# Side-by-side main and left keys, one softmax chain of 320 columns, and left outputs made once per group of four segments

## Chip, cores, metric

The kernel runs on 1 core of one Trainium2 chip. The metric is the device time of one execution in microseconds (us), as the median over several executions. The kernel before took 1781.87 us (median of 3 executions, 1777.33 to 1792.37).

## What is computed

Two branches of a transformer layer over 2048 rows of width 1024 are summed with the input: a recurrent attention over segments of 32 rows with a memory of 8 rows (A), and a dense layer with a gelu (B). Cut to what matters:

```python
def _A_ref(x, mem0, Wq, Wk, Wv, Wo, seg_len):         # x: 1 x 2048 x 1024, 32 heads of 128, M = 8, seg_len = 32
    mask = (idx[:, None] < M) | (idx[:, None] >= idx[None, :])
    mem = mem0
    for s in range(n_seg):                            # 64 segments, one after the other
        h = concat([mem, x[:, 32 * s:32 * s + 32]])   # 40 rows
        q, k, v = h @ Wq, h @ Wk, h @ Wv              # per head
        p = softmax(where(mask, q @ k.T * Dh ** -0.5, -1e9))
        o = (p @ v) @ Wo
        mem = o[:, :M]                                # goes into the next segment
        outs.append(o[:, M:])
    return concat(outs)

def _B_ref(x, w1, b1, w2, b2):                        # 1024 -> 3584 -> 1024
    return gelu(x @ w1 + b1) @ w2 + b2

return x + _A_ref(layernorm(x), ...) + _B_ref(layernorm(x), ...)
```

The memory makes the 64 segments a chain: a segment cannot start before the one ahead has given its 8 memory rows.

## The kernel before

**Two stages.** The first 340 us or so make the layer norm, branch B and, for each segment, its transposed rows in device memory. The rest of the span is the loop over 64 segments (`for s in range(NSEG)`), and all that the change touches at run time lies there.

**Rows of a segment.** A segment has 40 rows: 8 memory rows and 32 of its own. The kernel keeps 32 of them as *main* rows (24 own rows and the 8 memory rows, tile `hr_home`), since 32 rows fill one of four column groups of TensorE. The last 8 own rows are *left* rows. They don't depend on the memory, so those of four segments (a *group*; `GRP = 4`, `i4 = s % 4`) are put together to 32 rows (tile `hrL`) and projected once for the group.

**Weights.** Wq, Wk, Wv, Wo are cut into 64 units of 128 x 2048 (512 KB each): 8 for each half `u` of the heads of K, Q and V, and 16 of O. 47 stay in SBUF. 17 are streamed in each segment: 15 by DMA from device memory (`Wc_...`, issued by SP in `start_stream`, six buffers) and two that VectorE copies from PSUM (L273). `PLACED` fixes at which places of a segment's order of 64 units the streamed ones stand, one row of it for each `i4`. A buffer's next transfer is issued when its unit is done (`unit_done`).

**Products.** `half_pass` runs the eight units of one of the six halves, K0 Q0 K1 Q1 V0 V1, in this order. `product` (L830) sends a unit through TensorE as four matmuls of 512 columns, each with a stationary tile of 128 x 32 on its own column group; below this is called one *step*. A left projection adds a step to each unit of its half. Which segment has which left projection is in `left_k`, `left_q`, `left_v`. `o_product` (L1089) does the output projection: one step for each of the 16 O units, or two where left outputs are made as well (`left_o`: segments with `i4 == 1`, and the last one). In these, `left_outs` holds the left rows of four segments, two of the group ahead and two of this one (`og, slot = divmod(s + 2, GRP)`).

**Attention**, twice in a segment (`u` = 0, 1), its parts placed by hand between the units (`SCORES_0`, `SUMS_0`, `ATTEND`, `VALUES_0`, `SUMS_1`, `VALUES_1` give the unit behind which a part is issued):

- `scores`: 16 matmuls of main keys (L947) and 16 of left keys (L953), stationary 128 x 32, into two areas of one PSUM bank (`mixed`).
- `exps`: ScalarE's exp over 160 + 64 columns (L970 in one, or L966 and L967), then VectorE's minimum with two masks (L977, 96 and 64 columns).
- `sums`: eight matmuls with 0/1 columns `bd` (L985, L991), stationary 128 x 32; then on ScalarE ln of 160 columns (L996) and exp(-x) twice with two biases `off` (L999), which makes the two blocks of the 320 columns; then VectorE's products (L1012 for 320 columns, L1017 or L1024 for the left keys).
- `values`: 32 matmuls with stationary 64 x 128 (L1039, L1045), then copies out of PSUM (L1058).

**End of a segment.** `put_mem` (L320, stationary 128 x 128) turns the memory rows, VectorE copies them into the next segment's `hr_home` (L330). Up to six left steps of the next segment are issued around it (`lead_products`), so that TensorE has work meanwhile. The rows go out by small DMAs from POOL (L1273, L1276) and ScalarE.

**SBUF homes.** Keys of both halves share `nat_home` (in `d_oL`), left keys and left outputs lie in `ko`, the queries in `q_home` (in `kq`), which the values and the softmax also use in parts.

Of the kernel before, what the change touches and what calls it, by code (L numbers as in the profile page):

```python
# [33 lines left out]
NEVER = -30000.0  # L34
# [23 lines left out]
SCORES_0 = (6, 6, 6, 5)  # L58
# [62 lines left out]
def kernel(  # L121
# [57 lines left out]
    consts = ctx.enter_context(tc.tile_pool(name="consts", bufs=1))  # L179
# [4 lines left out]
    small_consts = consts.tile([P, 16], BF16, name="small_consts")  # L184
    bd, off = small_consts[:, 0:4], small_consts[:, 4:8].bitcast(F32)
# [9 lines left out]
    ident_mem = nc.alloc_sbuf_tensor_at("ident_mem", [P, 4, NL], BF16, offset=SCRATCH + 3712)[:, :, :]  # L195
    nc.vector.tensor_copy(out=ident_mem[:, :, :], in_=ident.rearrange("p (j t) -> p j t", j=4)[:, :, NX:SEG])
    nc.vector.memset(bd[:, :], 0.0)
    nc.vector.memset(off[:, :], NEVER)
    for j in range(4):
        q = slice(32 * j, 32 * j + 32)  # L200
        nc.vector.memset(bd[q, j:j + 1], 1.0)
        nc.vector.memset(off[q, j % 2:j % 2 + 1], 0.0)


    mask = qL[1].rearrange("p h t -> p (h t)")[:, 0:NX + GRP * 16]
    mask_order = mask[:, 0:NX]
    mask_left = mask[:, NX:].rearrange("p (g q) -> p g q", g=GRP)
    nc.gpsimd.memset(mask[:, :], PASSED)
    m = mask_order[0:NX, :]
# [3 lines left out]
    for half in range(2):  # L213
        m = mask_left[0:SEG, :, 8 - 8 * half:16 - 8 * half]
        nc.gpsimd.affine_select(
            out=m, in_=m, pattern=[[-8, GRP], [0, 8]], compare_op=ALU.is_ge, fill=0.0, base=0, channel_multiplier=1,
        )
        nc.gpsimd.affine_select(
            out=m, in_=m, pattern=[[8, GRP], [1 if half else 0, 8]], compare_op=ALU.is_ge, fill=0.0,
            base=0 if half else 7, channel_multiplier=-1,  # L220
        )

    def masks_out():
        for j in range(1, 4):
            nc.sync.dma_start(out=mask[32 * j:32 * j + 32, :], in_=mask[0:32, :])
# [74 lines left out]
    sp = ctx.enter_context(tc.tile_pool(name="sp", bufs=1))  # L300


    d_oL = sp.tile([P, 512 + 16 * 48], BF16, name="d_oL")
    kq = sp.tile([P, 16 * 48 + 672], BF16, name="kq")
    ko_flat = [d_oL[:, 512:], kq[:, 0:16 * 48]]
    ko = [t.rearrange("p (h t) -> p h t", h=16) for t in ko_flat]
    left_outs, left_keys = [t[:, :, 0:SEG] for t in ko], [t[:, :, 2 * NL:] for t in ko]
    q_all = kq[:, 16 * 48:]
    v_home = q_all[:, 0:512]
    outM = v_home.rearrange("p (h t) -> p h t", h=16)  # L310
    nat_home, q_home = d_oL[:, 0:512].rearrange("p (h t) -> p h t", h=16), q_all[:, 0:640].rearrange("p (h t) -> p h t", h=16)
# [37 lines left out]
    with tc.tile_pool(name="ma", bufs=2) as ma:  # L349
# [16 lines left out]
        o_sb = nat_home  # L366
# [97 lines left out]
        def keep_xT(tg, xnT):  # L464
            xl = [t[:, 0:512].rearrange("p (g k i t) -> p g k i t", g=2, k=KT, i=GRP) for t in ko_flat]
# [20 lines left out]
        def main_row(slot):  # L486

            return NL * slot + NL

        def with_left(seg):  # L490

            return seg % GRP == 1 or seg == NSEG - 1

        def turn_R(ttg, eng, small=None):
# [3 lines left out]
            for i in range(4):  # L498
                seg = 4 * ttg + i
                rows = R_n[seg * SEG:(seg + 1) * SEG, :].rearrange("t (j c) -> t j c", j=4)  # L500
                og, slot = divmod(seg + 2, GRP)
                both = [
                    t.rearrange("(h r) c -> r h c", h=2)
                    for t in (res_d[min(4 * og + 1, NSEG - 1) + 1, :, :], resL_d[og, :, :])
                ]
                halves = [rows.rearrange("t (h w) c -> t w h c", w=2)[:, w, :, :] for w in range(2)]
                if with_left(seg):
                    m0 = SEG
                    pairs = [(both[w][m0:m0 + SEG, :, :], halves[w]) for w in range(2)]
                else:  # L510
                    pairs = [(res_d[seg + 1, :, :].rearrange("(j t) c -> t j c", j=4), rows)]
                rows_at = [NL * slot]
                if seg < 2:
                    rows_at.append(NL * (slot ^ 2))
                elif seg >= NSEG - 2:
                    rows_at.append(2 * NL + NL * slot)
                for r0 in rows_at:
                    pairs += [(both[w][r0:r0 + NL, :, :], halves[w][NX:SEG, :, :]) for w in range(2)]
# [66 lines left out]
        for tg in range(4):  # L585
            last = tg == 3
            if last:

                load_x_rows(0)
                load_left_rows(0)  # L590
                h = 4 * IN_BANKS[1] + 2 * IN_BANKS[2]
                nc.sync.dma_start(out=kq[:, 0:DM], in_=Wo_v[:, h, :])
                start_stream("xn0")
                start_stream("xn1")
                fetch_resident("late2", "xt0", "xt1")
# [8 lines left out]
            for fb in range(FC):  # L604
# [18 lines left out]
                if last and fb == MEM_AT:  # L623
                    put_mem(o_sb, nxt["hT"], new_ps(), wide=False)
                    nc.sync.dma_start(out=d_oL[:, 0:DM], in_=Wo_v[:, h + 1, :])
# [110 lines left out]
    with tc.tile_pool(name="late", bufs=1) as late:  # L736
# [15 lines left out]
        def let_go(ps):  # L752
# [3 lines left out]
        trs = [  # L756
            mixed[:, 256 * n:256 * n + 256].bitcast(BF16).rearrange("p (c t) -> p c t", c=4) for n in range(2)
        ]
        there = mixed[:, 340:512].bitcast(BF16)
        qS = there[:, 0:32 * NL].rearrange("p (i h t) -> p i h t", i=2, h=16)  # L760
        masks_at = there[:, 32 * NL:32 * NL + NX + GRP * 16]
        mask_order = masks_at[:, 0:NX]
        mask_left = masks_at[:, NX:].rearrange("p (g q) -> p g q", g=GRP)
# [36 lines left out]
        kL, VL = [None] * 2, [None] * 2  # L800
        led = {}

        for s in range(NSEG):
# [12 lines left out]
            left_k = [first or (i4 == 3 and more), i4 == 0]  # L816
            left_q = [first or (i4 == 1 and more), first or (i4 == 2 and more)]
            left_v = [i4 == 0, first or (i4 == 3 and more)]
            left_o = i4 == 1 or final
            og, slot = divmod(s + 2, GRP)  # L820
            m0 = SEG if left_o else main_row(slot)
            st = {}

            def product(w, i, t, lhs, acc, seq):
                for j in range(4):
                    o, m = acc[32 * j:32 * j + 32, :], t[:, 512 * j:512 * j + 512]
                    if w != "V":
                        o = o.rearrange("p (h e) -> p h e", e=32)
                        m = t.rearrange("p (h q e) -> p q h e", q=4, e=32)[:, j, :, :]
                    nc.tensor.matmul(  # L830
# [8 lines left out]
            def lead_products(n):  # L839

                w, u, psL, ahead, order = led["next"]
                for _ in range(n):
                    if led["made"] < len(ahead):
                        i = ahead[led["made"]]
                        product(w, i, res_tiles[w, i, u], hL, psL, order)
                        led["made"] += 1

            def half_pass(w, u, left, at):
# [13 lines left out]
                for n in range(KT + lag):  # L862
# [7 lines left out]
                    if left and i not in ahead:  # L870
                        product(w, i, t, hL, psL, order)
# [8 lines left out]
            def rows_out(ps, out, cp):  # L880

                cp(out=out, in_=ps.rearrange("p (h e) -> p h e", e=32))  # L882
# [7 lines left out]
            def left_values(u, ps):  # L890
                VL[u] = values_out(ps, late.tile([P, 512], BF16, name=f"VL{u}"), nc.vector.tensor_copy)
# [6 lines left out]
            def turn_k(ps, u):  # L898
                st["kT", u] = nat_home
                turn(ps, nat_home, nc.scalar.copy)  # L900

            def turn_kL(ps, u):
                kL[u] = left_keys[u]
                turn(ps, kL[u], nc.vector.tensor_copy if first else nc.scalar.copy)
# [26 lines left out]
            def keep_q(u):  # L931
# [3 lines left out]
                    mixed[:, 340:340 + 64 * n].bitcast(U32).rearrange("p (i h t) -> p h i t", i=n, h=16),  # L935
# [3 lines left out]
            def scores(u):  # L939

                kT, qL_ends = st["kT", u], ends(q_home)
                sA = mixed[:, 0:160].rearrange("p (c q) -> p c q", q=40)
                sB = mixed[:, 160:224].rearrange("p (c q) -> p c q", q=16)
                for c in range(4):
                    for j in range(4):
                        q = slice(32 * j, 32 * j + 32)
                        nc.tensor.matmul(  # L947
                            sA[q, c, :], lhsT=kT[:, 4 * j + c, :], rhs=q_home[:, 4 * j + c, :],
                            start=(c == 0), stop=True, skip_group_check=True, tile_position=(0, 32 * j),
                        )  # L950
                    for j in range(4):
                        q = slice(32 * j, 32 * j + 32)
                        nc.tensor.matmul(  # L953
                            sB[q, c, :].rearrange("p (a b) -> p a b", b=NL), lhsT=kL[u][:, 4 * j + c, :],
                            rhs=qL_ends[:, 4 * j + c, :, :],
                            start=False, stop=True, skip_group_check=True, tile_position=(0, 32 * j),
                        )

            def exps(u):

                if u:
                    prA = q_all[:, 512:672].rearrange("p (c q) -> p c q", q=40)
                    c0 = 24 if i4 == 1 else 16
                    prB = ko[1][:, 0:8, c0:c0 + NL].rearrange("p (c a) q -> p c a q", a=2)
                    sB = mixed[:, 160:224].rearrange("p (c a q) -> p c a q", a=2, q=NL)
                    nc.scalar.activation(out=q_all[:, 512:672], in_=mixed[:, 0:160], func=ACT.Exp, scale=INV_SQRT_DH)  # L966
                    nc.scalar.activation(out=prB, in_=sB, func=ACT.Exp, scale=INV_SQRT_DH)  # L967
                else:
                    pr = q_all[:, 400:624]
                    nc.scalar.activation(out=pr, in_=mixed[:, 0:224], func=ACT.Exp, scale=INV_SQRT_DH)  # L970
                    prA = pr[:, 0:160].rearrange("p (c q) -> p c q", q=40)
                    prB = pr[:, 160:224].rearrange("p (c a q) -> p c a q", a=2, q=NL)
# [341 lines left out]
```

## Time and profile before

| what | value |
|---|---|
| median of 3 executions | 1781.87 us (1777.33 to 1792.37) |
| the profiled execution: its time / its span | 1788.29 us / 1786.6 us |
| TensorE (PE) matmul busy | 1697.1 us, 95% |
| VectorE (DVE) / ScalarE (ACT) / GpSimd (POOL) busy | 987.9 us, 55% / 670.5 us, 38% / 300.4 us, 17% |
| granted TensorE clock | 0.998 |
| DMA: bytes, mean rate | 594.37 MB, 333 GB/s |
| matmuls in the program | 30600 |
| first memory rows ready (L330) / last ones | 342.6 us / 1761.5 us |
| four segments in the middle of the loop | 85.0 us (847.3 to 932.3) |

The profile is of one execution, 0.4% above the median. "Busy" of PE is the time in which at least one matmul is under way, and a matmul of 512 columns is listed with 380 ns although the next step starts 0.216 us after it; so a busy PE can still be a waiting one, and the times at which matmuls start tell more than the busy share. Transfers, too, are nearly always under way in the loop.

### The profile page before, as it was taken

To read this page: it belongs to the slowest core of one execution; us is meant where nothing else is said; L and a number is where in the kernel's file an instruction comes from. 1 tells how busy PE (TensorE), PEld (TensorE's weight loads), DVE (VectorE), ACT (ScalarE), POOL (GpSimd) and SP (SyncE) were. 2 spreads that over 40 slices of the span, in tenths; PEclk is the share of its full clock that TensorE was granted. 3 is DMA by queue.
4 is the path that set the end of the run, shared out by engine and by line. 5 is a ranking of instruction groups with operands and counts; after the bars stand their busy time and mean duration, and the time that the engine had idled before them with its cause. 6 is when DMAs were issued, how large, how long until landed. Compare 5 with 4: busy or idle time off the path is not lost.

```text
span 1786.6 us, 70503 instructions
## 1 busy us (share of the span) xinstructions
PE 1697.1 (95%) x30600; PEld 867.5 (49%) x30600; DVE 987.9 (55%) x2642; ACT 670.5 (38%) x1709; POOL 300.4 (17%) x586
## 2 busy tenths in 40 slices
PE   9999999998999999999999999999999999999988
PEld 5444444444445544444545444454445445445444
DVE  7657483825555555555555555555555555555544
ACT  6334251603333333333333333343334333333333
POOL 0000002401231111111121211111121111111111
PEclk9999999999999999999999999999999999999999
DMA  9455312779999999999999999999999999999998
GB/s 278 146 167 169 91 45 71 267 277 335 387 390 388 387 374 383 380 383 367 393 378 382 374 381 393 389 388 389 375 387 400 389 389 394 380 378 396 378 376 316
DMA packets 232827, 594.37 MB, mean 333 GB/s; under 512 B 57715, under 2 KB 88035, under 8 KB 232516
## 3 DMA queue, kind: packets, MB, share of 16 engines
q1 hardware_dynamic: 197584, 567.08, 84.3%
q0 software_dynamic: 16896, 16.85, 2.8%
q10 hardware_dynamic: 18036, 5.94, 1.3%
q8 instruction: 239, 3.92, 0.9%
q14 instruction: 72, 0.59, 0.1%
HBM read 573.43 MB, written 28.90 MB: 337 GB/s over the span
## 4 chain that ended last, share of the span: by engine, by line
PE 70%; DMA 18%; DVE 4%; issue 3%; ACT 3%; ACTq 1%; SPq 1%; DVEq 0%
PE acc L830 36%; PE acc L1089 11%; PE ps L534 10%; DMA u<-Wc_O 10%; PE ps L662 6%; DMA u<-Wc_V 5%; PE ps L693 3%; PE acc L1039 1%; ACTq L459 1%; ACT mixed L999 1%; PE mixed L947 1%; SPq L521 1%; DMA hr_home<-res_d 1%; DVE pd_main L1012 1%; PE mixed L320 1%
## 5 line engine op out<-in xcount | busy, mean ns | idle before, releaser
L830 PE MATMUL acc<-u,hr_home 128*32 128x512 bf16 x11520 | 763.6, 380 | 19.7 <-DMA u<-Wc_V 10.2
L830 PEld LDWEIGHTS <-hr_home 128*32 128x32 bf16 x12288 | 337.8, 96 | 303.2 <-issue 45.2
L830 PE MATMUL acc<-u,hrL 128*32 128x512 bf16 x2880 | 253.0, 382 | 4.0 <-DMA hrL<-rowsL_d 2.1
L534 PE MATMUL ps<-u 128*128 128x512 bf16 (+1 forms) x992 | 195.1, 358 | 0.4 <-DMA u<-in_B_w_dram 0.4
L273 DVE TENSOR_SCALAR u<-kept 128x512 uint32<-128x512 uint32 x254 | 163.1, 684 | 48.0 <-PE acc L830 40.6
L1089 PE MATMUL acc<-u,d_oL 128*32 128x512 bf16 x2592 | 170.4, 380 | 13.0 <-issue 10.2
L882 ACT CAST d_oL<-acc 128x512 bf16<-128x512 f32 x143 | 82.0, 584 | 253.9 <-PE acc L830 220.9
L662 PE MATMUL ps<-u 128*128 128x512 bf16 x672 | 146.0, 379 | 0.0
L534 PEld LDWEIGHTS <-u 128*128 128x128 bf16 x992 | 91.6, 98 | 102.1 <-DMA u<-in_B_w_dram 0.6
L1089 PE MATMUL acc<-u,kq 128*32 128x512 bf16 (+1 forms) x2696 | 132.4, 320 | 8.1 <-DMA u<-Wc_O 6.4
L1012 DVE TENSOR_TENSOR pd_main<-kq,mixed 128x320 bf16<-128x320 bf16 x128 | 62.5, 488 | 129.2 <-ACT mixed L999 129.2
L909 ACT CAST kq<-acc 128x256 bf16<-128x256 f32 x256 | 89.4, 375 | 109.7 <-PE acc L830 76.6
L1089 PEld LDWEIGHTS <-kq 128*32 128x32 bf16 x3344 | 87.4, 96 | 84.0 <-ACT kq L1058 24.2
L1276 POOL DMA_DIRECT2D out_dram<-hr_home x168 | 85.4, 516 | 220.5 <-DVE hr_home L1243 220.5
L913 DVE STREAM_TRANSPOSE kq<-kq 128x256 bf16<-128x256 bf16 x256 | 98.2, 422 | 42.8 <-ACT kq L909 42.7
L886 ACT CAST kq<-acc 128x512 bf16<-128x512 f32 x128 | 75.2, 588 | 114.1 <-PE mixed L953 111.7
L977 DVE TENSOR_TENSOR kq<-kq,mixed 128x96 bf16<-128x96 bf16 (+1 forms) x256 | 38.1, 190 | 143.8 <-ACT kq L967 87.2
L830 PEld LDWEIGHTS <-hrL 128*32 128x32 bf16 x3072 | 86.3, 96 | 58.4 <-issue 3.7
L662 PEld LDWEIGHTS <-u 128*128 128x128 bf16 x672 | 65.5, 98 | 78.8 <-DVE u L619 0.4
L611 ACT ACTIVATE u<-ps,b1col 128x512 bf16<-128x512 f32 x112 | 76.5, 684 | 64.5 <-PE ps L534 61.7
L1089 PEld LDWEIGHTS <-d_oL 128*32 128x32 bf16 x2592 | 64.0, 96 | 69.5 <-issue 23.5
L999 ACT ACTIVATE mixed<-mixed,small_consts 128x160 f32<-128x160 f32 x256 | 94.2, 368 | 8.4
(127 smaller groups left out, 1910.5 us busy)
## 6 DMA issues: line engine op xcount, KB each, us to landing
u<-Wc_K SPq DMA_DIRECT2D x256, 512.0 KB
u<-Wc_V SPq DMA_DIRECT2D x256, 512.0 KB
u<-Wc_O SPq DMA_DIRECT2D x256, 512.0 KB
u<-Wc_Q SPq DMA_DIRECT2D x192, 512.0 KB
u<-in_B_w_dram SPq DMA_DIRECT2D x28, 512.0 KB
u<-in_A_Wq_dram SPq DMA_DIRECT2D x13, 512.0 KB
u<-in_A_Wv_dram SPq DMA_DIRECT2D x12, 512.0 KB
u<-in_A_Wk_dram SPq DMA_DIRECT2D x9, 512.0 KB
```

What stands on the lines that cost most here:

```text
L273: nc.vector.tensor_single_scalar(out=out, in_=in_, scalar=0, op=ALU.bitwise_or)
L534: nc.tensor.matmul(ps[:, SEG * s0:SEG * s1].rearrange("p (s t) -> p s t", t=SEG), lhsT=w1_sb[fb // 2][:, kt, (fb % 2) * P:(fb % 2 + 1) * P ...
L611: nc.scalar.activation(out=xb[:, :], in_=ps[:, :], func=ACT.Identity, bias=b1col[:, fb:fb + 1], scale=1.0)
L662: nc.tensor.matmul(ps[:, :], lhsT=gts[fc // 4][:, fc % 4, t * P:(t + 1) * P], rhs=w2_sb[fc // 2][:, fc % 2, cs], start=(fc == 0), stop=(fc ...
L830: nc.tensor.matmul(o, lhsT=lhs[:, i, :], rhs=m, start=(i == seq[0]), stop=(i == seq[-1]), tile_position=(0, 32 * j),)
L882: cp(out=out, in_=ps.rearrange("p (h e) -> p h e", e=32))
L909: nc.scalar.copy(out=q_home[:, h0:h1, NL:40], in_=ps[:, 32 * h0:32 * h1].rearrange("p (h e) -> p h e", e=32))
L913: nc.vector.transpose(out=half, in_=half)
L999: nc.scalar.activation(out=mixed[:, 160 * b:160 * b + 160], in_=mixed[:, 0:160], func=ACT.Exp, scale=-1.0, bias=off[:, b:b + 1],)
L1012: nc.vector.tensor_tensor(out=pdA.rearrange("p c b q -> p b c q"), in0=prA[:, None, :, :].to_broadcast([P, 2, 4, 40]), in1=dd, op=ALU.mult,)
L1089: nc.tensor.matmul(acc[r0:r0 + rows, 0:256 * len(blocks)], lhsT=lhsT, skip_group_check=True, rhs=o_columns(t, k, blocks), start=start, sto ...
L1276: loads.dma_start(out=out_flat[rows, 256 * j:256 * j + 256], in_=res[32 * j:32 * j + NX, :])
```

## The change

Memory for keys and outputs becomes two tiles `both[u]` of 1024 columns, in which each pair of heads has 128 columns: left, main, main, left (32 each). Main and left of one head thus stand side by side.

- `scores`: one matmul for main and left keys of a head, stationary 128 x 64, 40 columns, 16 instead of 32; each two run on two column groups. The scores take 320 columns of `mixed`.
- `exps`: one exp of 320 columns; then three minima: two of 64 columns, which also take the left keys' part out, and one of 320 columns.
- `sums`: four matmuls with stationary 64 x 64 (row halves and column halves), 320 and 128 columns, instead of eight; ln and exp(-x) once each over 320 columns; two products.
- Left outputs are made in segments with `i4 == 3` for the group itself, 16 times instead of 17. There, the first head of each pair is one matmul with stationary 128 x 64 for left and main; the second, whose two parts stand the other way round, stays with 128 x 32.
- Left K of half 0 moves from `i4 == 3` to `i4 == 0`, and the lead products ahead of segment `i4 == 3` become those of V1. Left values have two fixed tiles in turn, without the copy L1191.
- Masks are built in another form, with six instead of three small transfers at the start; `SCORES_0` of `i4 == 3` goes from 5 to 6. `PLACED` is as it was.

In steps, the left work of the four segments of a group goes from 16, 24, 8, 16 to 24, 8, 8, 24. The program has 27478 matmuls instead of 30600.

```diff
-SCORES_0 = (6, 6, 6, 5)
+SCORES_0 = (6, 6, 6, 6)
...
-    d_oL = sp.tile([P, 512 + 16 * 48], BF16, name="d_oL")
-    kq = sp.tile([P, 16 * 48 + 672], BF16, name="kq")
...
+    both_flat = [sp.tile([P, DM], BF16, name=f"both{u}") for u in range(2)]
+    both = [t.rearrange("p (n w) -> p n w", w=128) for t in both_flat]
+    quarters = [t.rearrange("p (n q t) -> p n q t", q=4, t=SEG) for t in both_flat]
+    main_of, left_of = [t[:, :, 1:3, :] for t in quarters], [t[:, :, ::3, :] for t in quarters]
+    q_all = sp.tile([P, 640], BF16, name="q_all")
...
-            left_k = [first or (i4 == 3 and more), i4 == 0]
+            left_k = [i4 == 0, i4 == 0]
...
-            left_o = i4 == 1 or final
-            og, slot = divmod(s + 2, GRP)
+            left_o = i4 == 3
+            VL = [VLs[(g + u) % 2] for u in range(2)]
...
             def scores(u):
-                sA = mixed[:, 0:160].rearrange("p (c q) -> p c q", q=40)
-                sB = mixed[:, 160:224].rearrange("p (c q) -> p c q", q=16)
+                S = mixed[:, 0:320].rearrange("p (c b q) -> p c b q", b=2, q=40)
                 for c in range(4):
-                    for j in range(4):
...
+                    for b in range(2):
+                        for r in range(2):
+                            n = 2 * c + r
+                            nc.tensor.matmul(
+                                S[64 * r:64 * r + 64, c, b, :], lhsT=both[u][:, n, 64 * b:64 * b + 64],
+                                rhs=q_home[:, 2 * n + b, :],
+                                start=(c == 0 and b == 0), stop=True, skip_group_check=True,
+                                tile_position=(0, 64 * r),
+                            )
 
             def exps(u):
...
+                nc.scalar.activation(
+                    out=pr, in_=mixed[:, 0:320].rearrange("p (n q) -> p n q", q=40), func=ACT.Exp, scale=INV_SQRT_DH
+                )
+                by_head = pr.rearrange("p (c b) q -> p c b q", b=2)
+                for a in range(2):
+                    m = ...
+                    nc.vector.tensor_tensor(
+                        out=prL.rearrange("p (c b a q) -> p c b a q", c=4, b=2, a=2)[:, :, :, a, :],
+                        in0=by_head[:, :, :, SEG * a:SEG * a + NL], in1=m.to_broadcast([P, 4, 2, NL]), op=ALU.min,
+                    )
+                nc.vector.tensor_tensor(
+                    out=by_head, in0=by_head, in1=mask_order[:, None, :, :].to_broadcast([P, 4, 2, 40]), op=ALU.min
+                )
...
+            def sums(u):
+                pr, prL = st["pr", u]
+                d = mixed[:, 0:320].rearrange("p (n q) -> p n q", q=40)
+                for r in range(2):
+                    q = slice(64 * r, 64 * r + 64)
+                    nc.tensor.matmul(
+                        d[q, :, :], lhsT=ones_col[q, :].to_broadcast([64, 64]), rhs=pr[q, :, :],
+                        start=True, stop=False, skip_group_check=True, tile_position=(64 * r, 64 * r),
+                    )
...
+                nc.scalar.activation(out=mixed[:, 0:320], in_=mixed[:, 0:320], func=ACT.Ln)
+                nc.scalar.activation(out=mixed[:, 0:320], in_=mixed[:, 0:320], func=ACT.Exp, scale=-1.0)
+                nc.vector.tensor_tensor(
+                    out=pd_main.rearrange("p (n q) -> p n q", q=40), in0=pr, in1=d, op=ALU.mult
+                )
...
             def o_product(n, t, acc):
...
                     if left_o:
-                        lhs = [(0, 32, left_outs[i // 4][:, h, :]), (32, 32, main)]
+                        lhs = [(0, 32, left_of[i // 4][:, n_of, k, :]), (32, 32, main)]
+                        if k == 0:
+                            lhs = [(0, 64, both[i // 4][:, n_of, 0:64])]
                         tiles = [(64 * r + r0, w, (2 * r, 2 * r + 1), lhsT) for r0, w, lhsT in lhs for r in range(2)]
...
-            def moved_values():
-
-                VL[1] = late.tile([P, 512], BF16, name="VL1")
-                (nc.vector if s < EARLY_SEGS else nc.gpsimd).tensor_copy(out=VL[1].rearrange("p (h t) -> p h t", t=SEG), in_=ahead_v)
-
...
-                    w, u = (("Q", 0), ("Q", 1), ("K", 0), ("K", 1))[i4]
+                    w, u = (("Q", 0), ("Q", 1), ("V", 1), ("K", 0))[i4]
```

288 lines of the change are left out of this document (104 added, 184 removed).

## The prediction, as put on record

> **What bounds the kernel now.** I read the page first (busy shares, DMA), then the four segments of one group by windows, then who TensorE (PE) waits for, then PE's timeline around each kind of matmul.
>
> ```profile
> PE 1697.1 (95%) x30600; PEld 867.5 (49%) x30600; DVE 987.9 (55%) x2642; ACT 670.5 (38%) x1709; POOL 300.4 (17%) x586
> DMA  9455312779999999999999999999999999999998
> ```
>
> PE and the 16 DMA engines are both nearly always busy in the loop. Segments 20 to 23 (`i4` 0 to 3), as span, PE, PEld, DVE, ACT, POOL busy, clock, DMA share, GB/s:
>
> ```profile
> 847.30:867.80 20.50, 19.83 (x458) 12.89 (x450) 11.98 (x34) 8.04 (x23) 3.71 (x7) 1.00 1.02 402
> 867.80:889.80 22.00, 21.50 (x476) 11.20 (x468) 10.62 (x30) 7.77 (x22) 3.71 (x7) 1.00 1.02 394
> 889.80:910.20 20.40, 18.36 (x426) 9.70 (x418) 12.58 (x34) 7.58 (x22) 4.71 (x9) 1.00 1.02 385
> 910.20:932.30 22.10, 20.29 (x458) 10.74 (x450) 11.27 (x32) 8.74 (x24) 3.79 (x7) 1.00 0.99 365
> sum 85.00, PE 79.97 PEld 44.53 DVE 46.44 ACT 32.13 POOL 15.91; mean PE 19.99 PEld 11.13 DVE 11.61 ACT 8.03 POOL 3.98
> ```
>
> A group takes 85.0 us. Its mean rate is 386 GB/s, so it moves 32.8 MB; at the best window's 402 GB/s that is 81.7 us. The transfers are thus a floor only 3.3 us under the present time, while PE has no more than 5 us idle. VectorE and ScalarE are half idle and count only where PE waits for one of their results. PE's waits over the run:
>
> ```profile
> PE mixed L953 <- issue: 11.2, 12, 2.0
> PE acc L1089 <- issue: 10.5, 15, 1.3
> PE acc L830 <- DMA u<-Wc_V: 10.2, 20, 1.1
> PE acc L1089 <- DMA u<-Wc_O: 8.7, 22, 0.8
> PE acc L1039 <- DVE pd_main L1012: 5.9, 23, 0.3
> ```
>
> Transfers (18.9 us in these two rows) and "issue" (21.7) lead; the softmax chain is a small third. So PE time counts nearly one for one when it is added, and can gain little when it is taken away. Now what PE does when the shape of the stationary tile changes:
>
> ```profile
> 877.65 0.62 PE L830 MATMUL acc<-u,hr_home 128*32 128x512 bf16 x8
> 878.09 0.21 PE L947 MATMUL mixed<-kq,d_oL 128*32 128x40 bf16 x4
> ...
> 878.27 0.23 PE L953 MATMUL mixed<-kq 128*32 128x16 bf16 x4
> 878.34 1.14 PE L830 MATMUL acc<-u,hr_home 128*32 128x512 bf16 x16
> 879.41 0.21 PE L1039 MATMUL acc<-pd_main,kq 64*128 64x80 bf16 x2
> ...
> 879.64 0.18 PE L1045 MATMUL acc<-d_oL,VL 64*128 64x32 bf16 x2
> 879.75 1.02 PE L830 MATMUL acc<-u,hr_home 128*32 128x512 bf16 x12
> 880.58 0.25 PE L985 MATMUL mixed<-kq,small_consts 128*32 128x160 bf16 x4
> ...
> 880.68 0.40 PE L1089 MATMUL acc<-u,d_oL 128*32 128x512 bf16 x4
> ```
>
> ```profile
> 888.74 0.60 PE L830 MATMUL acc<-u,hrL 128*32 128x512 bf16 x8
> 889.28 0.26 PE L320 MATMUL mixed<-ident_mem,kq 128*128 128x16 bf16 x4
> 889.47 0.40 PE L830 MATMUL acc<-u,hrL 128*32 128x512 bf16 x4
> ```
>
> A step of four matmuls of 512 columns lasts 0.38 us, but the next one starts 0.217 us behind it (a row of 40 at 871.10 lasts 2.33 us: 1.95 / 9). The last step ahead of L947 starts at 877.65 + 0.62 - 0.38 = 877.89, and L947 0.20 later: same shape, no loss; nor on the way back (878.34). The last step ahead of L1039 starts at 878.34 + 1.14 - 0.38 = 879.10, and L1039, of another shape, 0.31 later: 0.10 lost. Back again, L830 starts 0.11 us after the last L1045, where pairs of the same shape come 0.03 apart: 0.08 lost. L320 shows the same: 888.96 to 889.28 (0.10 lost), and its last at about 889.37, L830 at 889.47 (0.07 lost). So **a change of the stationary tile's shape empties PE's pipeline: 0.10 us behind a step of 512 columns, 0.07 behind a short matmul, 0.17 for there and back.** Scores and sums now have the shape of the projections and pay nothing.
>
> **The change part by part**, per group of four segments.
>
> *Scores* (8 stretches): now 8 lots of four in 0.25 us (878.09 to 878.34). Afterwards 8 pairs of 64 columns' width: at 0.025 a lot (L947) to 0.036 (L1039's pairs) that is 0.20 to 0.29; I take no difference. But 128 x 64 among steps of 128 x 32 is another shape: 8 x 0.17 = +1.4. No row has exactly this pair; the rows nearest to it (to 128 x 128, to 64 x 128) both lose, so I take it in full and keep 0 as the low end. The Trainium skill, "TensorEngine Tiling (Array Packing)", section Tiling Modes, lists 128 x 64 and 128 x 32 as different configurations and says that a change of tiling mode drains TensorE; by it the full sum holds, and its two visible cases agree with the rows above.
>
> *Sums* (8): now 0.10 us (880.58 to 880.68). Afterwards 320 and 128 columns instead of 160 and 64: 448 / 512 x 0.217 = 0.19, so +0.09, and another shape, +0.17: 8 x 0.26 = +2.1.
>
> *Left outputs*: in `i4 == 3`, each of 16 units goes from 128 x 32 to 128 x 64 and back, both behind 512 columns: 16 x 2 x 0.10 = +3.2 (low end 0). Fewer matmuls (six for eight) save nothing, since those on different column groups run side by side. One left segment less: -16 x 0.217 = -3.5 once in the run.
>
> *Softmax chain.* Exp of 320 columns: from L966 (160: 309 ns) and L970 (224: 358) 0.77 ns a column, 0.43 us; +0.07 for `u` = 0, nothing for `u` = 1 (L966 and L967 overlap: 0.42). Minima: 0.20 + 0.18 (L977) become 0.18 + 0.18 + 0.4 (320 columns, between L977's 0.20 and L1012's 0.49): +0.38. So sums are ready 0.45 and 0.38 us later. From the end of L977 to L985 there are now, by `i4`, 0.44, 0.13, 0.56, 0.54 us (`u` = 0) and 0.30, 0.78, 0.98, 1.14 (`u` = 1), of which 0.1 is needed and `SCORES_0` takes one step, 0.22, in `i4` 3. New waits: 0.11 + 0.42 + 0 + 0.23 and 0.18: +0.9. Behind the sums, L996 and two L999 (0.29 + 0.77) become 0.42 + 0.45: 0.2 earlier, which shortens L1039's waits in `i4` 0 and 2 (0.25 each): -0.4. Net +0.5 (0 to +0.9). Queued behind the longer minima on VectorE are the key transposes (L1135), needed five steps later. The new home of the softmax in the first half of the queries makes the first copy of `turn_q` wait for the product; the second one waits for it already, and the chain to the second scores ends as late as now.
>
> *Instructions.* A tenth fewer matmuls and weight loads. The "issue" waits (11.2 + 10.5, and 6.0 and 4.0 in smaller rows) come to 31.7 us; with a tenth less I take -3 over the run, -0.2 per group; the low end is all of them.
>
> *Hidden.* Six mask transfers instead of three on SP's queue (now three in 3.8 us, up to 16.2 us) delay the weights behind them by 4 us; the first of these are issued at 18.05 and used at about 32 us. POOL and ScalarE lose a handful of small DMAs. The copy L1191 was off the path.
>
> *Cover.* PE's waits for transfers (18.9, and 2.1 for L273's copies) are 21.0 us in 44 waits, each with 0.16 more that the listed 0.38 us hides: 28 us, 1.8 per group. The group's bytes stay, its time grows by more than this, so these waits go: -1.8 (high end: none goes). The uneven left work (24, 8, 8, 24 steps) is bridged by six buffers: the two short segments need 2 x 15 transfers of 1.3 us, 39 us, and last about 40.
>
> Sum per group: 1.4 + 2.1 + 3.2 + 0.5 - 0.2 - 1.8 = **+5.2 us**; 16 groups, less 3.5: **+80 us**. The profiled execution took 1788.3, so 1868 for one like it; it lies 0.36% above the median, so against 1782 I say **1862 us** (own range 1825 to 1890: chain at 0 and all "issue" gone, or no cover).
>
> **Rivals.**
> *Row halves in one bank.* The new sums send two row halves into one PSUM bank; L1039's pairs, which start together, write two banks. If they go one after the other: 0.19 more, 8 x 0.19 x 16 = +24: 1886. For it: no row shows two row halves in one bank. Against: column groups share a bank at no cost (L985). The Trainium skill, same page, section Restrictions and Gotchas, says that row tiles cannot access one bank at the same time.
> *Width alone costs nothing*: column groups change independently, only the sums' row halves drain. Then 2.1 + 0.5 - 0.2, half of the cover: +1.5 x 16 - 3.5 = +20: 1802. Against: L320 changes only the columns, and loses.
> *Hidden by the transfers*: without drains at all, sums' +0.7 and +0.5 vanish in the cover: 1785.
> *The other side, instruction supply*: the trace has an instruction queue (239 packets), and "issue" waits sit where small matmuls are densest. With half the scores' instructions all 31.7 us go, with 0.16 for each of 42 waits 38 us; if also no shape drains: 1782 - 38 + 5 - 3.5 = 1745. It decides only while PE's additions stay under 2 us per group.
> *Pairs of 64 not side by side* in the left outputs: 16 x 0.217 more per group: 1918.
>
> **Chances.** Forecast 0.49, row halves 0.18, width alone 0.15, hidden 0.08, instruction supply 0.05, pairs 0.05. The range 1790 to 1895 leaves out the last three, 0.18. Within 1% (1764 to 1800) is about what a measurement of this kernel can tell from no change. Faster by over 1%: 0.05. Within: 0.08 and a third of width alone: 0.13. Slower: 0.82.
>
> **What would show it.** Right: segments of about 23, 19.5, 20.5 and 27.5 us; in `i4` 3 each O unit 0.63 instead of 0.43 us; L830 to the scores 0.31 instead of 0.21 us; PE's waits for `Wc_` nearly gone; DMA share clearly under 1 in `i4` 3 and 0. Wrong: scores that follow a step by 0.21 us, or four windows with sum 85.

## The result and the profile after

The changed kernel takes 1856.43 us (median of 4 executions, 1856.19 to 1859.42), the kernel before 1781.59 us (median of 4) on the same chip. The ratio is 1.0414, with a 95% interval from 1.0367 to 1.0462: slower by 75 us. The profiled execution has a span of 1854.1 us against 1786.6.

From the page of the changed kernel, the busy shares and the DMA row (40 slices, tenths):

```profile
PE 1797.3 (97%) x27458; PEld 838.1 (45%) x27478; DVE 1020.5 (55%) x2696; ACT 647.9 (35%) x1517; POOL 285.5 (15%) x567
DMA  9564314889999999999999999999999999999997
```

A tenth fewer matmuls, and PE is busy 100 us longer. The clock is 0.999, so the matmuls are not slower; they stand further apart. The same group of four segments as before (20 to 23, `i4` 0 to 3), by windows, with the columns of the prediction's table:

```profile
867.98:890.55 22.57, 22.37 (x450) 10.88 (x442) 13.34 (x37) 8.24 (x21) 5.24 (x10) 1.00 0.93 321
890.55:911.58 21.03, 19.31 (x386) 9.50 (x378) 12.45 (x36) 7.26 (x19) 3.16 (x6) 1.00 1.02 399
911.58:931.34 19.76, 19.11 (x382) 9.22 (x374) 12.53 (x36) 7.26 (x19) 3.14 (x6) 1.00 1.02 402
931.34:957.49 26.15, 26.15 (x404) 10.98 (x400) 9.97 (x30) 7.96 (x20) 3.69 (x7) 1.00 0.91 349
sum 89.51, PE 86.93 PEld 40.58 DVE 48.30 ACT 30.72 POOL 15.23; mean PE 21.73 PEld 10.15 DVE 12.07 ACT 7.68 POOL 3.81
```

85.0 us have become 89.5. Two segments are as short as the transfers allow (DMA share 1.02, 399 and 402 GB/s); in the other two the transfers have room (0.93, 0.91), and the one with the left outputs has grown most. PE's waits in the changed kernel:

```profile
PE acc L1056 <- DMA u<-Wc_O: 25.3, 48, 1.1
PE acc L819 <- DMA u<-Wc_V: 5.2, 13, 1.1
PE mixed L321 <- DVE q_all L1172: 5.2, 16, 1.0
PE acc L819 <- DMA hrL<-rowsL_d: 2.9, 1, 2.9
```

No row says "issue" any more, where before had 31.7 us. The waits for transfers are still there: 35.1 us in all rows, before 21.4. (L819 is the product, L1056 the output projection, L937 the scores, L968 and L974 the sums, L1005 and L1011 the values, L321 `put_mem`.)

PE's timeline in `i4 == 1`, around the scores and the sums:

```profile
899.69 1.70 PE L819 MATMUL acc<-u,hr_home 128*32 128x512 bf16 x28
901.31 0.43 PE L937 MATMUL mixed<-q_all,both 128*64 128x40 bf16 x16
901.67 1.05 PE L819 MATMUL acc<-u,hr_home 128*32 128x512 bf16 x16
...
902.99 0.83 PE L819 MATMUL acc<-u,hr_home 128*32 128x512 bf16 x12
903.75 0.32 PE L968 MATMUL mixed<-both,between 64*64 64x320 bf16 x2
903.91 0.22 PE L974 MATMUL mixed<-q_all,between 64*64 64x128 bf16 x2
904.06 0.83 PE L1056 MATMUL acc<-u,both 128*32 128x512 bf16 x12
```

The last step ahead of L937 starts at 899.69 + 1.70 - 0.38 = 901.01; the scores follow 0.30 later (0.319 as the median of all such pairs in the loop, where a step follows a step by 0.217). The sums follow theirs by 903.75 - (902.99 + 0.83 - 0.38) = 0.31. Both are the 0.10 us that the prediction read off L1039 and L320. Then, in `i4 == 3`, the left outputs, four units in each row of 24:

```profile
949.45 2.74 PE L1056 MATMUL acc<-u,both 128*64 128x512 bf16 x24
952.11 1.40 PE L1056 MATMUL acc<-W_O,both 128*64 128x512 bf16 x12
953.45 2.74 PE L1056 MATMUL acc<-u,both 128*64 128x512 bf16 x24
```

952.11 - 949.45 = 2.66 us for four units, 0.665 each. Two undisturbed steps would take 0.43. By the starts of single matmuls, the way from 32 to 64 columns' width costs 0.330 and the way back 0.336, instead of 0.217: 0.23 lost per unit, 16 x 0.23 = 3.7 us in one segment.

**Where a group's time goes.** From the starts of PE's matmuls in the trace, segments 8 to 59 (13 groups), each interval between the starts of two successive steps (called a stretch where other work lies between them) is put under what lies between them. A step counts 0.217 us (0.108 for 256 columns); the other rows hold what an interval has beyond this. All in us per group:

| | before | after | after, all three in 128 x 32 (`a_all32`) |
|---|---|---|---|
| steps | 70.0 | 69.5 | 69.5 |
| stretches with scores | 3.3 | 3.75 | 2.1 |
| stretches with sums or values | 6.1 | 7.85 | 8.1 |
| `put_mem` | 1.5 | 1.4 | 1.2 |
| shape changes between two steps, and other short gaps | 0.8 | 4.4 | 0.9 |
| waits between two steps | 3.6 | 2.6 | 4.2 |
| sum | 85.35 | 89.45 | 85.95 |

Before and in `a_all32` no two successive steps differ in shape, so what stands there in the row of shape changes, 0.8 and 0.9 us, are other short gaps, most of them of 0.2 us in the output projection. The changes of shape alone are 3.6 us, in the changed kernel only. After less before is 4.1: +3.6 from the left outputs' shape, +1.8 from sums and values together, +0.4 from the scores, and -1.6 from waits, `put_mem` and steps that were pulled apart (the parts are rounded). 15.75 groups make 64.6 us, the start 1 and the last segment, which also makes left outputs, 5: 70, where the spans differ by 67.5 (the 13 groups stand for all of them here). The medians differ by 75, because the profiled execution of before was 6 us above its own median.

### The profile page after: what moved, and what is told of

Same layout as the page of the kernel before. It is cut to its first block, busy times and chain, and to the rows that moved or that the text cites. A ratio compares the mean times of both kernels' runs of the same rounds, so it can differ in the third digit from the quotient of the medians.

```text
span 1854.1 us, 64138 instructions
## 1 busy us (share of the span) xinstructions
PE 1797.3 (97%) x27458; PEld 838.1 (45%) x27478; DVE 1020.5 (55%) x2696; ACT 647.9 (35%) x1517; POOL 285.5 (15%) x567
## 4 chain that ended last, share of the span: by engine, by line
PE 76%; DMA 20%; DVE 1%; ACTq 1%; issue 1%; ACT 1%; SPq 0%; DVEq 0%
PE acc L819 37%; PE acc L1056 14%; DMA u<-Wc_O 11%; PE ps L526 10%; PE ps L654 6%; DMA u<-Wc_V 4%; PE ps L685 3%; DMA u<-Wc_Q 2%; PE mixed L937 2%; DMA u<-Wc_K 1%; PE mixed L968 1%; PE acc L1005 1%; ACTq L460 1%; DMA hrL<-rowsL_d 1%; PE mixed L321 1%
## 5 line engine op out<-in xcount | busy, mean ns | idle before, releaser
L819 PE MATMUL acc<-u,hr_home 128*32 128x512 bf16 x11520 | 761.4, 380 | 7.8 <-DMA u<-Wc_V 5.2
L819 PEld LDWEIGHTS <-hr_home 128*32 128x32 bf16 x12288 | 314.1, 96 | 313.6 <-issue 42.4
L1056 PE MATMUL acc<-u,both 128*32 128x512 bf16 (+2 forms) x4800 | 341.5, 350 | 26.9 <-DMA u<-Wc_O 25.3
L1056 PEld LDWEIGHTS <-both 128*32 128x32 bf16 (+1 forms) x5376 | 153.8, 96 | 220.1 <-issue 146.8
L819 PE MATMUL acc<-u,hrL 128*32 128x512 bf16 x2880 | 248.0, 380 | 4.4 <-DMA hrL<-rowsL_d 2.9
L871 ACT CAST both<-acc 128x512 bf16<-128x512 f32 x158 | 89.5, 586 | 250.2 <-PE acc L819 212.7
L1023 DVE CAST both<-acc 128x64 bf16<-128x64 f32 (+1 forms) x256 | 70.7, 318 | 95.4 <-PE acc L1011 95.2
L904 DVE STREAM_TRANSPOSE q_all<-q_all 128x256 bf16<-128x256 bf16 x256 | 98.7, 424 | 42.0 <-ACT q_all L900 38.3
L900 ACT CAST q_all<-acc 128x256 bf16<-128x256 f32 x256 | 82.8, 375 | 110.5 <-PE acc L819 73.5
L879 ACT CAST q_all<-acc 128x512 bf16<-128x512 f32 x128 | 75.3, 589 | 96.3 <-PE mixed L937 95.3
L819 PEld LDWEIGHTS <-hrL 128*32 128x32 bf16 x3072 | 79.5, 96 | 62.5 <-DMA hrL<-rowsL_d 3.6
L1023 ACT CAST both<-acc 128x64 bf16<-128x64 f32 (+1 forms) x256 | 62.3, 295 | 115.6 <-PE acc L1011 115.6
L978 ACT ACTIVATE mixed<-mixed 128x320 f32<-128x320 f32 x128 | 54.0, 422 | 97.4 <-PE mixed L974 91.1
L889 DVE STREAM_TRANSPOSE both<-both 128x512 bf16<-128x512 bf16 x96 | 65.9, 698 | 17.4 <-ACT both L871 17.0
L1142 POOL DMA_DIRECT2D hr_home<-res_d x57 | 31.7, 556 | 280.1 <-PE acc L819 209.1
```

Of the source, the lines that this page charges most:

```text
L819: nc.tensor.matmul(o, lhsT=lhs[:, i, :], rhs=m, start=(i == seq[0]), stop=(i == seq[-1]), tile_position=(0, 32 * j),)
L871: cp(out=out, in_=ps.rearrange("p (n b e) -> p n b e", b=2, e=32) if len(out.shape) == 4 else ps.rearrange("p (h e) -> p h e", e=32),)
L879: cp(out=t[:, :], in_=ps[:, :])
L900: nc.scalar.copy(out=q_home[:, h0:h1, NL:40], in_=ps[:, 32 * h0:32 * h1].rearrange("p (h e) -> p h e", e=32))
L904: nc.vector.transpose(out=half, in_=half)
L1023: cp(out=out, in_=oV[r][:, :, :, q0:q1])
```

## Experiments

All kernels were timed beside the kernel before on the same chip; its medians there were 1782.2 to 1782.8 us. "Undone" always means: the operation again with a stationary tile of 128 x 32, as in the steps around it.

### Left outputs alone in 128 x 32 (`a_o32`)

```diff
-                        if k == 0:
-                            lhs = [(0, 64, both[i // 4][:, n_of, 0:64])]
```

> The changed kernel, but in the left segments every output matmul has a 128 x 32 stationary tile again (eight for a unit instead of six, all in one shape). Theory of the shape change: a unit falls from 0.33 + 0.34 to 0.43 us, 16 units x 16 segments x 0.23 = -60 us, some of it given back to transfers: 1796 to 1816. Rival of the uneven work (left work of 24, 8, 8, 24 steps starves and floods the six buffers, the shapes cost little): under 10 us gained, 1846 or more.

Measured 1800.76 us, ratio 1.0097 (1.0059 to 1.0136): 56 us less than the changed kernel. PE's timeline, eight matmuls to a unit, and the window of this segment:

```profile
931.27 1.91 PE L1054 MATMUL acc<-u,both 128*32 128x512 bf16 x32
933.01 1.04 PE L1054 MATMUL acc<-W_O,both 128*32 128x512 bf16 x16
```

```profile
914.58:937.10 22.52, 22.52 (x436) 10.92 (x432) 10.05 (x29) 7.96 (x20) 3.69 (x7) 1.00 1.02 393
```

933.01 - 931.27 = 1.74 us for four units, 0.435 each: 32 more matmuls in the segment, and it is 3.6 us shorter. 16 groups with 3.5 are the 56 us, three quarters of the whole change.

### Half of the left outputs' shape changes (`a_alt`)

```diff
-                for k in range(2):
+                for k in ((1, 0) if left_o and n % 2 else (0, 1)):
```

The matmuls are the same, wide ones too; every second unit takes its two heads in the other order, so that 64 follows 64 and 32 follows 32.

> The changed kernel with the same matmuls, but in the left segments odd O units make the 128 x 32 head first and the 128 x 64 head second, so that two units share each change of shape: 16 changes in a left segment instead of 32. Theory of the shape change (0.12 us each as the changed kernel's steps show): 16 x 16 x 0.12 = -30 us: 1826. Rival: 128 x 64 tiles are slow in themselves (weight load, pairs not side by side): no change, 1856.

Measured 1831.28 us, 1.0278 (1.0247 to 1.0309): 25 us less, nearly half of 56. The left outputs of segment 23 (the first four units, and the two behind them):

```profile
941.85 2.39 PE L1056 MATMUL acc<-u,both 128*64 128x512 bf16 x24
944.07 1.26 PE L1056 MATMUL acc<-W_O,both 128*64 128x512 bf16 x12
```

944.07 - 941.85 = 2.22 us for four units, 0.555 each, in the middle between 0.665 and 0.435. A wide pair behind a wide pair starts after 0.240 us (median), little more than a narrow step's 0.217. So it is the change of shape that costs and not the wide matmul.

### The left outputs' shape put into the kernel before (`b_o64`)

```diff
                     if left_o:
                         lhs = [(0, 32, left_outs[i // 4][:, h, :]), (32, 32, main)]
+                        if k == 0:
+                            f = v_home if i >= 4 else nat_home.rearrange("p h t -> p (h t)")
+                            lhs = [(0, 64, f[:, 32 * h:32 * h + 64])]
```

> The kernel before with one part of the change alone: in left segments (i4 = 1 and the last) the first head of each pair is multiplied with 128 x 64 stationary tiles (neighbouring columns, so the left outputs are not the reference's), the second with 128 x 32. Theory of the shape change: 17 x 16 x 0.23 = +63 us, less the waits for transfers that these segments have there (0.6 us each, 10 us): 1830 to 1845. Rival: it costs only together with the changed layout or place: under 1800.

Measured 1836.48 us, 1.0309 (1.0283 to 1.0336): +54 us. Segment `i4 == 1`, where before makes its left outputs, goes from a mean of 22.5 to 25.7 us. There, two units take 903.14 - 901.81 = 1.33 us, 0.665 each as in the changed kernel:

```profile
901.81 1.40 PE L1092 MATMUL acc<-W_O,kq 128*64 128x512 bf16 x12
903.14 2.74 PE L1092 MATMUL acc<-u,kq 128*64 128x512 bf16 x24
```

The price is thus nearly the same from both sides, 54 us added in 17 segments and 56 taken away in 16, and needs nothing else of the change.

### Scores alone, sums alone, and all three in 128 x 32 (`a_s32`, `a_m32`, `a_all32`)

Scores, four matmuls on four column groups for two on two:

```diff
-                        for r in range(2):
-                            n = 2 * c + r
+                        for j in range(4):
+                            n, w = 2 * c + j // 2, 32 * (j % 2)
...
-                                S[64 * r:64 * r + 64, c, b, :], lhsT=both[u][:, n, 64 * b:64 * b + 64],
+                                S[32 * j:32 * j + 32, c, b, :], lhsT=both[u][:, n, 64 * b + w:64 * b + w + 32],
...
-                                tile_position=(0, 64 * r),
+                                tile_position=(0, 32 * j),
```

> The changed kernel, but scores are made by 32 matmuls with 128 x 32 stationary tiles into the same 320 columns. Shape change: a stretch of scores falls from 0.68 to about 0.46 us, 128 x 0.22 = -28 us, less what transfers take back: 1828 to 1840; if the number of instructions is what removed the waits on issue, some of those come back here. Uneven work: 1850 or more.

Measured 1856.12 us, 1.0409 (1.0376 to 1.0442): no gain. Sums with the same columns, but columns of 0 and 1 over all 128 rows:

```diff
-                for r in range(2):
-                    q = slice(64 * r, 64 * r + 64)
+                for j in range(4):
+                    q = slice(32 * j, 32 * j + 32)
...
-                        d[q, :, :], lhsT=ones_col[q, :].to_broadcast([64, 64]), rhs=pr[q, :, :],
-                        start=True, stop=False, skip_group_check=True, tile_position=(64 * r, 64 * r),
+                        d[q, :, :], lhsT=halves_of_ones[j // 2].to_broadcast([P, 32]), rhs=pr,
+                        start=True, stop=False, skip_group_check=True, tile_position=(0, 32 * j),
```

> The changed kernel, but sums are made by eight matmuls with 128 x 32 stationary tiles of zeros and ones (320 and 128 columns as in the changed kernel). Shape change: of 0.63 us the 0.10 behind the last step and about 0.1 on the way back go, 0.40 stays: 128 x 0.22 = -28 us: 1828 to 1840. If the two row halves were run one after the other in one bank, more is gained: under 1820. Uneven work: 1850 or more.

Measured 1852.59 us, 1.0381 (1.035 to 1.0412): 4 us less, within the intervals. The two edits and that of `a_o32` together:

> The changed kernel with all three kinds in 128 x 32 tiles: same layout, same softmax chain of 320 columns, same places of the left work. Shape change: -60 - 28 - 28 = 1740 at best, the transfers' floor of 81.7 us a group is near 1735; I expect 1750 to 1785, so no slower than the kernel before. Uneven work: over 1830.

Measured 1798.02 us, 1.0083 (1.0048 to 1.0118). What I expected of the shapes missed in all three, and in the same way. The first two times lie where the rival, the uneven work, put them (1850 or more), but that rival asked for over 1830 in `a_all32` as well, and 1798 rules it out as the main cause. As it is, the shapes of scores and sums are worth nothing beside that of the left outputs. The local price is there all the same. By the accounting above, the scores' row falls from 3.75 to 2.2 us per group in `a_s32`, and sums and values from 7.85 to 6.9 in `a_m32`. But the first gives 1.1 back in the row of sums and values and 0.6 in waits between steps; the second gives 0.9 back in the waits. Two rows of `a_s32` name what comes out:

```profile
PE acc L819 <- issue: 3.0, 4, 0.9
PE mixed L968 <- DVE q_all L958: 2.6, 14, 0.2
```

"Issue" is back (7.7 us in all rows), and the sums now wait for the minima (L958). In `a_m32` the waits for transfers rise from 35.1 to 44.3 us, in `a_all32` to 48.2.

### Fewer transfers, in both kernels (`a_less`, `b_less`)

To see PE without waits for transfers, both kernels leave out four of the 15 transfers of a segment; these units are multiplied with a tile that is already in SBUF. "Without the transfers" means these kernels below:

```diff
+SKIP = (("K", 5, 1), ("V", 4, 0), ("O", 3, 0), ("O", 6, 1))
...
+            if unit in SKIP:
+                return res_tiles[RESIDENT[0]]
```

> The changed kernel with four of the fifteen transfers of a segment left out (these units are multiplied with a resident tile instead, so those products are not the reference's). Without a full queue, PE's own time shows. Waits for transfers (35 us listed, about 45 with what the listed duration hides) should nearly go: about 1810. If transfers were the bound: under 1780.

> The kernel before with the same four transfers left out. Waits for transfers go (28 us): 1754 if the waits on issue stay, as they would if it were the number of instructions that makes them; about 1716 if these too come from a full transfer queue. The distance to the changed kernel without these transfers is PE's own extra time: 128 x (0.22 + 0.31) + 256 x 0.23 = 128 us by its stretches, less 10 for shorter softmax waits: 90 to 120 if nothing hides it.

Measured: `a_less` 1833.02 us, 1.0282 (1.0252 to 1.0312), 23 less than with the transfers; `b_less` 1750.97 us, 0.9824 (0.9789 to 0.9859), 31 less than before. The changed kernel gets less out of it than I expected (23 for 46), and the distance between the two is 82 us, less than the 90 to 120 of the expectation. Five rows of PE's waits in `b_less`:

```profile
PE mixed L957 <- issue: 7.5, 8, 1.6
PE acc L1043 <- ACT kq L886: 6.5, 14, 0.5
PE acc L834 <- issue: 6.3, 6, 1.6
PE mixed L951 <- issue: 6.2, 6, 2.1
PE acc L1093 <- issue: 6.2, 9, 1.2
```

All waits for weights are gone, and 26.2 us of "issue" stay. They do not come from a full transfer queue, as one theory had it: the DMA share is 0.85 here (400 to 1750 us). `a_less` has none, and no wait for a weight either.

### Shapes undone without the transfers (`a_less_s32`, `a_less_m32`, `a_less_all32`)

The edits of above, made in `a_less`.

> The same for scores: four transfers left out, scores in 32 matmuls of 128 x 32. Theory: the stretch gets 0.19 us shorter, but the minima then end later than TensorE arrives at the sums (0.16 us in one of two) and waits on issue come back, of which the kernel before has 26 us without these transfers: between 1815 and 1835, and issue waits of 5 to 25 us. Rival, only transfers took the gain: 1833 - 25 = 1808 with no waits on issue.

Measured 1825.47 us, 1.024 (1.0216 to 1.0264): 8 us less than `a_less`.

> The changed kernel with four transfers of a segment left out (as in the run that took 1833; those products are not the reference's) and sums in 128 x 32 tiles. With all transfers this edit shortened a stretch of sums by 0.17 to 0.2 us and the run by only 4. Theory: the gain was lost to waits for transfers, so without them it shows: 128 x 0.21 = -27 us: 1806. Rival: the sums' change of shape lies beside other work anyway (the softmax chain): 1828 to 1833.

Measured 1820.44 us, 1.0213 (1.0192 to 1.0234): 13 us less, between the two expectations.

> Four transfers left out, all tiles 128 x 32. With all transfers this form was 16 us slower than the kernel before (1798 to 1782). Theory: that rest is the uneven left work, which only costs by way of the transfers; without them it should equal the kernel before in the same condition: 1751 plus or minus 8. Rival: the softmax chain of 320 columns is slower in itself: 1760 to 1770.

Measured 1755.69 us, 0.9844 (0.9819 to 0.9869), 5 above `b_less`, and the intervals overlap. So even without the transfers the drains of scores and sums are worth less than they measure. Per group, by the same accounting: in `a_less_s32` the scores' row falls by 1.6 us, the row of sums and values rises by 0.8 and the waits between steps by 0.3 (5.4 us of "issue" are back in the run); in `a_less_m32` the sums' stretches fall by 1.3, the values' rise by 0.4 and the scores' by 0.1. What takes most of the gain is the softmax chain. Scores that end sooner reach the sums before the minima are done (a sums' stretch of 0.635 on the mean in `a_less`, 0.731 in `a_less_s32`), and sums that end sooner reach the values before the products are. One row each of PE's waits, of `a_less_s32` and of `a_less_m32`, which `a_less` does not have:

```profile
PE mixed L972 <- DVE q_all L962: 2.8, 15, 0.2
```

```profile
PE acc L1012 <- DVE pd_main L987: 4.8, 16, 0.3
```

A drain and a wait for the chain lie in the same time, and only the longer counts. With 32 changes in one output phase, in which nothing has to be waited for, no such cover exists.

### Uneven left work in the kernel before (`b_uneven`)

```diff
-            left_k = [first or (i4 == 3 and more), i4 == 0]
+            left_k = [i4 == 0, i4 == 0]
...
-            left_o = i4 == 1 or final
+            left_o = i4 == 3
...
-                    w, u = (("Q", 0), ("Q", 1), ("K", 0), ("K", 1))[i4]
+                    w, u = (("Q", 0), ("Q", 1), ("V", 1), ("K", 0))[i4]
```

> The kernel before with the changed kernel's places of the left work: left outputs in the segments with i4 = 3 (16 times), left K of half 0 in i4 = 0, lead products of V1; tiles, softmax chain and layout stay as before. What goes into the left outputs' slots is no longer the right group's data. The changed kernel with all tiles 128 x 32 took 1798, 16 more than before. Theory of the uneven work (24, 8, 8, 24 steps): it is this, transfers that PE waits for in the short segments: 1792 to 1805. Rival, the softmax chain of 320 columns is the rest: 1775 to 1785, since one left segment less saves 3.5.

Measured 1791.3 us, 1.0052 (1.0034 to 1.007): +9 us, just under the range of the theory that the uneven work costs (the nearer one). PE's waits for transfers rise from 21.4 to 46.1 us, much as in `a_all32`; its "issue" waits fall from 31.7 to 5.5, though the program has nearly the same matmuls (30550, before 30600). The two longest rows:

```profile
PE acc L1089 <- DMA u<-Wc_O: 27.6, 58, 1.3
PE acc L830 <- DMA u<-Wc_V: 12.3, 27, 1.1
```

## Why the prediction was right, and where not

The forecast was 1862 us, the measurement 1856. The mechanism that it rests on is shown, but the number came so close in part by luck. In the prediction's sum, scores and sums stand for +56 us over the run, the left outputs for +51, and all the rest (chain, instructions, cover, one left segment less) for -28. Undoing the left outputs gave 56 us, undoing scores and sums besides only 3 more, and 16 are left above before. So one part of the sum was 53 us too high and another 44 too low, and these two errors nearly cancel.

**A change of the stationary tile's shape drains PE: right, in its price too.** 0.10 us behind a step of 512 columns was read off two places of the trace of before; afterwards it is 0.10 at scores and sums and 0.11 to 0.12 between two steps. That a change of width alone costs as much was open: 32 to 64 columns does (0.330 against 0.217). The Trainium skill, "TensorEngine Tiling (Array Packing)", section Tiling Modes, lists the two as different configurations and says that a change of tiling mode drains TensorE. By the 0.330 us the trace agrees. The rivals "Width alone costs nothing", "Hidden by the transfers" and "Instruction supply" fall with it, the last although its waits did go. "Pairs of 64 not side by side" falls with 0.665 us a unit, which has room for two steps and two drains and for no third step. (The 1785 us given for "Hidden by the transfers" fits an execution like the profiled one, 1788.3 - 3.5; against the median the sum is 1782 - 3.5 = 1778.)

**Row halves in one bank: fell.** L974 starts 0.159 us behind the two L968 of 320 columns (median). 320 columns at 0.217 / 512 need 0.136 us, two in turn 0.27. So the two halves ran side by side. The Trainium skill, same page, section Restrictions and Gotchas, says that different row tiles cannot access one PSUM bank at the same time. Here they did, on different partitions of it, and the measurement decides.

**Left outputs, +3.2 per group: 3.7 by the timeline, 3.5 by what undoing them gave.** This one term is three quarters of the result, where the prediction had it as less than half of what it added (3.2 of 7.2).

**Scores +1.4 and sums +2.1: the local price is right, its worth to the run is not.** The stretch around the scores grew from 0.458 to 0.681 us (median, 8 x 0.22 = 1.8 per group) and that around the sums from 0.313 to 0.628 (8 x 0.31 = 2.5). Undoing them one at a time gave 0 and 4 us, where the two terms stand for 16 x 3.5 = 56. The step that failed is the sentence that PE time counts nearly one for one when it is added: it does in the second half of `i4 == 3`, not where the queue of transfers, the minima or an "issue" wait is next in line. The two halves of that segment show the difference:

```profile
931.34:945.00 13.66, 13.66 (x264) 6.66 (x260) 7.23 (x22) 5.52 (x15) 2.59 (x5) 1.00 1.03 400
945.00:957.49 12.49, 12.49 (x144) 4.32 (x140) 2.74 (x8) 2.44 (x6) 1.10 (x2) 1.00 0.78 293
```

In the first the transfers run at their full share (1.03), and PE's time there is time they need; in the second they are at 0.78, ahead of PE, and every 0.1 us of PE lengthens the run. That is read from the shares; the runs without the transfers bear it out in part, where undoing scores and sums gave 8 and 13 us instead of 0 and 4.

**Cover, -1.8: mis-sized, with the wrong sign.** PE's waits for transfers did not go; the listed ones grew by 13.7 us, +0.9 per group. A group has the time for its transfers on the whole, but the segments with `i4` 1 and 2, of 20.6 and 19.9 us on the mean, have not, and six buffers do not carry over what the long ones gain: 25.3 us of waiting for `Wc_O`, of which 25.1 lie in these two. The prediction worked out that they would ("39 us, and last about 40") with the mean of 1.3 us a transfer and nothing to spare; that line failed. `b_uneven` shows these waits without the shapes.

**Instructions, -0.2: mis-sized.** All 31.7 us of "issue" went, -2.0 per group, the low end of the range given. But the reason, a tenth fewer matmuls, is not what decides: `b_uneven` and `a_less_all32` have nearly as many as before (30550 each, before 30600, and the same 239 packets of the instruction queue) and 5.5 and 1.9 us of "issue".

**Softmax chain, +0.5: hidden in the changed kernel, there without the drains.** No wait for the minima is listed there. In `a_all32`, with no drains left at scores, sums and left outputs, sums and values take 8.1 us per group against 6.1 before; 8 x 0.095 = 0.8 of it are the longer rows (448 columns for 224), and 1.2 is left, against the +0.5 of the sum. I put it down to PE's waits on a chain that is longer by its minima (2.5 us are listed at the sums, and the listed durations of the steps ahead hide a part of each wait); no run separates it further.

**Left over.** `a_all32` is still 16 us above before. Without the transfers this shrinks to 5: there the chain takes back what the lost "issue" waits give (2.2 us per group for the scores' row in `a_less_all32` against 3.8 in `b_less`, 8.2 for sums and values against 6.55). With the transfers, 9 of the 16 are those of the uneven left work alone. The other 7 are not settled. None of the kernels that do the whole work beat the one before.

Of the signs named, these came: segments of 22.6, 20.6, 19.9 and 26.4 us on the mean (foretold about 23, 19.5, 20.5, 27.5), 0.665 a unit (0.63), 0.32 to the scores (0.31), and the DMA share under 1 in `i4` 3 and 0. Waits for `Wc_` nearly gone did not come.

## What to carry to other kernels

Before merging matmuls, list the shape of the stationary tile of each against its neighbours: 32 fewer matmuls in a segment cost 3.6 us because each wide one stood alone among narrow ones, and ordering them by shape won half of it back. A local price read off the timeline is worth its full size only where the other queues are ahead at that point; take the DMA share of that stretch (0.78 or 1.03) and the next result in the chain before multiplying. When transfers bound the loop, look at the shortest segment, not at the group's sum.

## Not expected of the hardware

- Two matmuls of 64 x 64 on opposite halves of rows and columns, which write different partitions of one PSUM bank, ran side by side: 0.159 us for 320 columns.
- "Issue" waits of PE come and go with things that are not the count of matmuls or instruction packets: 31.7 us before, 26.2 with 27% fewer weight transfers, 5.5 with the left work in other segments, none with 64-column scores. In this record every kernel whose scores are 128 x 32 has some, and none of the six whose scores are 128 x 64 has any; what sets them is open all the same.
